# K transposed on TensorE for 48 units instead of 32, in halves through two PSUM banks

## The chip, the cores and the metric

The kernel runs on one core of a Trainium2 chip. The metric is the device time of that core in microseconds (us). Before the change three runs gave 1071.03, 1072.39 and 1073.0 us, a median of 1072.39; the profiled execution took 1071.12 us, with a profiled span of 1069.4 us at a granted TensorE clock of 0.999.

## The reference

Two attention blocks of the same shape, A and B, follow one another; their outputs stand side by side in the last dimension. For each block, with 16 batches, 16 heads, 144 query rows, 448 model columns, 512 cached keys and a head width of 256, all bf16:

```
q = (x @ wq) as 16 heads of 256 columns
scores = q @ k_cache^T / 16          for each batch and head
p = softmax(scores)
o = p @ v_cache
out = (o of the 16 heads, side by side) @ wo
```

## The kernel before

The work is cut into units: one unit is one batch and one head, 256 units for A and 256 for B, numbered through (U). A unit has 512 keys, 256 KB of K and 256 KB of V. Scores are computed with the keys on the partitions, so K is needed with the head width on the partitions, that is transposed, while V is used as it lies in memory.

One loop over i emits everything; in step i it emits, in this order,

- `t_tr(i+4)`: the transposes of K on TensorE, only for the first NNAT * UV = 32 units. Eight 128 x 128 transposes write one PSUM bank, `op_ps` seen as bf16 (`tr_ps`); then VectorE copies the first half and ScalarE the second half into `kt_sb` (L973). All three name the bank "op".
- `t_q(i+3)` and `t_evac_q(i+3)`: the Q projection (L1005) into `qp_ps`, two banks under the one name "qp", and its copy by VectorE into a slot of `qt_sb`. `q_pair` says for how many batches a unit's Q is made at once: 2 (288 columns, for this batch and the next), 1 (144 columns) or 0 (already made).
- `t_s(i+2)`: scores (L1038), in two halves of two key blocks, into one of three banks `s_ps` in turn; ScalarE takes the exp of each half (L1048) into `pt_sb`.
- `t_pv(i)` and `t_sum(i)`: the product with V (L1083) and the row sums by a matmul with ones (L1095), in one of two banks `ot_ps`. The sums come from partial sums that GpSimd made two steps earlier (`t_presum`, L1058 and L1062).
- `t_recip(i)` on ScalarE (a logarithm, L1106, and an exp, L1111), and on VectorE `t_check(i)` (two reductions over the sums, L1140) and `t_evac_ot(i)` (L1126), which scales the result into `ring`.
- pieces of the output projection (`t_op_piece`, L1182) into `op_ps`, from step 28 on (`OP_START`), at a rate that a running credit sets.

Each engine executes its own instructions in the order in which they were emitted. `_Sched.add` derives the waits: an operation waits for the last writers of what it reads, for the readers of what it overwrites, and, for each PSUM bank it names, for the last operation of every *other* engine on this bank:

```
        for bk in banks:
            last = self.banks.setdefault(bk, {})
            for e2, ev2 in last.items():
                if e2 != eng:
                    deps.append(ev2)
```

So two engines never work on one bank at the same time; whichever was emitted later waits.

All loads go through one queue, SyncE's, in an order that is written out for the first units (`START`, in which n, v, k, q, o and x stand for natural K of two units, V of two units, transposed K of 16 units, a part of wq, a part of wo, a group of x) and planned after it. Natural K (`t_load_n`, L954) and V (`t_load_v`, L946) share the nine slots of `v_sb`, two units in each; a load waits until the load nine places earlier has been used. Transposed K (`t_load_k`, L933) is a transposing DMA of 16 units, a window, into one of the two halves of `kt_sb`; window W holds units 16W to 16W + 15. A window's load waits until the scores of the units that lay there before are done. In the kernel before, windows 0 and 1 are made on TensorE and all from window 2 on come by transposing DMA.

Of the kernel before, what the change touches and what calls it, by code (L numbers as in the profile page):

```python
# [5 lines left out]
BF16 = mybir.dt.bfloat16  # L6
F32 = mybir.dt.float32
I32 = mybir.dt.int32
AF = mybir.ActivationFunctionType
# [3 lines left out]
PE, ACT, DVE, POOL, SP = "pe", "act", "dve", "pool", "sp"  # L13
# [739 lines left out]
def bass_concat_heads__mha_block_cached__gqa_block_cached__near_ridge_kernel(  # L753
# [16 lines left out]
    ins = (A_x, A_k_cache, A_v_cache, A_wq, A_wo, B_x, B_k_cache, B_v_cache, B_wq, B_wo)  # L770
# [6 lines left out]
    Bn, SQ, D = A_x.shape  # L777
    H, SK, DH = A_k_cache.shape[1], A_k_cache.shape[2], A_k_cache.shape[3]
# [4 lines left out]
    UV = 2  # L783
# [3 lines left out]
    NWO = 2 * H  # L787
# [5 lines left out]
    LQ, LS, LT = 3, 2, 4  # L793
    KW, KR = 16, 32
    NV, NXG = 9, 2
    NNAT = KR // UV
    assert KR % KW == 0 and NU % KW == 0
    XB = 4
    assert Bn % (NXG * XB) == 0 and H == KW
    NQT, NPT, NPS, NRI, NOST, NRUN = 11, 3, 2, 2, 2, 32  # L800
# [5 lines left out]
    LIM_EXP = 40  # L806


    START = ("n0 q0 x0 n1 v0 n2 v1 q1 n3 v2 n4 v3 n5 q2 n6 v4 n7 v5 o0 q3 n8 v6 n9 v7 o1 n10 v8 o2 n11 v9 n12 v10 "
             "n13 v11 n14 v12 n15 v13 v14 k2 v15 o3 v16 v17 o4 o5 v18 o6 v19 o7 v20 v21 v22 x1 k3")  # L810
    MID = ("k16 v127 v128 q0 v129 v130 q1 v131 q2 q3 v132 k17 v133 v134 v135 v136 v137 o0 o1 v138 o2 v139 o3 v140 o4 v141 "
           "o5 v142 o6 o7 k18")

# [2 lines left out]
    with contextlib.ExitStack() as es:  # L816
# [8 lines left out]
        wq_sb = sb("wq_sb", [128, 4, H * DH], BF16)  # L825
        wo_sb = sb("wo_sb", [128, NWO, D], BF16)
        ring = sb("ring", [128, NWO, RC], BF16)
        kt_sb = sb("kt_sb", [128, 8, KR * 128], BF16)
        v_sb = sb("v_sb", [128, NV, UV, 4 * DH], BF16)
        xt_sb = sb("xt_sb", [128, 4, NXG * XB * SQ], BF16)  # L830
        qt_sb = sb("qt_sb", [128, NQT, 2, SQ], BF16)
        pt_sb = sb("pt_sb", [128, NPT, 4, SQ], BF16)
        ones = sb("ones", [128, 128], BF16)
# [8 lines left out]
        qp_ps = ps("qp_ps", [128, 2, 512], F32)  # L842
        s_ps = [ps("s_ps%d" % i, [128, 512], F32) for i in range(3)]
        ot_ps = [ps("ot_ps%d" % i, [128, 512], F32) for i in range(2)]
        op_ps = ps("op_ps", [128, 512], F32)
        tr_ps = op_ps[:, :].bitcast(BF16)
        ident = ring[:, NWO - 1, 2 * 128:3 * 128]

        S = _Sched()
        sem_names = list(COMPUTE)  # L850
# [14 lines left out]
        def unit(U):  # L865
            pr, r = divmod(U, NU)
            b, h = divmod(r, H)
            return pr, b, h

        def t_init():  # L870
            def e0(v):
                return v.memset(stat[:, 0:2], 0.0)
            S.add(DVE, e0, writes=[("scr", 0)], name="statz")

            def e1(a):
                a.preload_act_table_set("natural_log_exp_and_others")
                return a.activation(stat[0:1, 1:2], stat[0:1, 0:1], AF.Exp)
            S.add(ACT, e1, reads=[("scr", 0)], writes=[("scr1", 0)], name="actwarm")

            def e2(v):  # L880
                return v.memset(wq_sb[0:64, 3, :], 0.0)
            S.add(DVE, e2, writes=[("wqz", 0)], name="wqz")

            def e4(g):
                return g.memset(ones[:], 1.0)
            S.add(POOL, e4, writes=[("ones", 0)], name="ones")

            def e5(g):
                return g.affine_select(ident, ones[:], pattern=[[1, 128]], compare_op=ALU.is_equal,
                                       fill=0.0, base=0, channel_multiplier=-1)  # L890
            S.add(POOL, e5, reads=[("ones", 0)], writes=[(("ring", 2, H - 1), -1)], name="ident")
            for W in range(NNAT * UV // KW):
                S.res[(("kt", W))] = _Res()
                S.res[(("kt", W))].version = W

        def t_load_wq(pr, hg):
            cols = slice(hg * 4 * DH, (hg + 1) * 4 * DH)
# [56 lines left out]
                return q.dma_start(v_sb[:, sl, :, :], src).then_inc(sems["v%d" % sl], 16)  # L954
            S.add(SP, e, writes=[(("v", sl), ("n", G))], dma_sem="v%d" % sl, name="n%d" % G)

        def t_tr(U):
            G, j = divmod(U, UV)
            sl = v_seq["n", G] % NV
            ko = U % KR * 128  # L960

            def e(t):
                ins = None
                for k in range(8):
                    ins = t.transpose(tr_ps[:, k * 128:(k + 1) * 128], v_sb[:, sl, j, k * 128:(k + 1) * 128], ident)  # L965
                return ins
            S.add(PE, e, reads=[(("v", sl), ("n", G)), (("ring", 2, H - 1), -1)], writes=[("opp", ("t", U))],
                  banks=["op"], name="TR%d" % U)
            for k, eng in ((0, DVE), (1, ACT)):
                def ev(g, k=k, eng=eng):  # L970
                    dst = kt_sb[:, 4 * k:4 * k + 4, ko:ko + 128]
                    src = tr_ps[:, k * 512:(k + 1) * 512].rearrange("p (c q) -> p c q", c=4)
                    return g.activation(dst, src, AF.Copy) if eng == ACT else g.tensor_copy(dst, src)  # L973
                S.add(eng, ev, reads=[("opp", ("t", U))], writes=[(("ktn", U % KR), 0)], banks=["op"],
                      name="etr%d.%d" % (U, k))

        def q_pair(U):

            b, h = unit(U)[1:]
            if h % 2 == 0:  # L980
                return 2 if b % 2 == 0 else 0
            j = b % (NXG * XB)
            return 1 if j in (0, NXG * XB - 1) else (2 if j % 2 else 0)

        q_slot, q_live = {}, {}
        for U in range(NT):
            for u in [u for u in q_live if u - LS < U - LQ]:
# [5 lines left out]
        def t_q(U):  # L993
            pr, b, h = unit(U)
            n = q_pair(U)
            xo = b % (NXG * XB) * SQ
            xr = sorted(set((pr * Bn + b + k) // XB for k in range(n)))
            hg = h // 4

            def e(t):  # L1000
                ins = None
                for dc in range(2):
                    for kc in range(4):
                        c0 = h * DH + dc * 128
                        ins = t.matmul(qp_ps[:, dc, 0:n * SQ], lhsT=wq_sb[:, kc, c0:c0 + 128],  # L1005
                                       rhs=xt_sb[:, kc, xo:xo + n * SQ], start=(kc == 0), stop=(kc == 3))
                return ins
            S.add(PE, e, reads=[(("wq", hg), pr), ("wqz", 0)] + [(("xt", XG % NXG), XG) for XG in xr],
                  writes=[("qp", ("q", U))], banks=["qp"], name="Q%d" % U)

        def t_evac_q(U):
            n = q_pair(U)
            us = [U + k * H for k in range(n)]
            a, b = q_slot[us[0]], q_slot[us[-1]]

            def e(v):
                if n == 1:
                    return v.tensor_copy(qt_sb[:, a, :, :], qp_ps[:, :, 0:SQ])  # L1018
                return v.tensor_copy(qt_sb[:, a:b + 1:b - a, :, :],  # L1019
                                     qp_ps[:, :, 0:2 * SQ].rearrange("p e (u q) -> p u e q", u=2))  # L1020
            S.add(DVE, e, reads=[("qp", ("q", U))], writes=[(("qt", q_slot[u]), u) for u in us], banks=["qp"],
                  name="eq%d" % U)

        def t_s(U):
            W = U // KW
            ksl = W % (KR // KW)
            ko = U % KR * 128
            qsl = q_slot[U]
            kn = [(("ktn", U % KR), 0)] if U < NNAT * UV else []
            psl = U % NPT  # L1030
            for k in range(2):
                bank = (2 * U + k) % 3

                def e(t, k=k, bank=bank):
                    ins = None
                    for c in (2 * k, 2 * k + 1):
                        for dc in range(2):
                            ins = t.matmul(s_ps[bank][:, (c % 2) * SQ:(c % 2 + 1) * SQ],  # L1038
                                           lhsT=kt_sb[:, 2 * c + dc, ko:ko + 128],
                                           rhs=qt_sb[:, qsl, dc, :], start=(dc == 0), stop=(dc == 1))  # L1040
                    return ins
                S.add(PE, e, reads=[(("qt", qsl), U), (("kt", ksl), W)] + kn, writes=[(("sp", bank), 2 * U + k)],
                      banks=["s%d" % bank], name="S%d.%d" % (U, k))
            for k in range(2):
                bank = (2 * U + k) % 3

                def x(a, k=k, bank=bank):
                    return a.activation(pt_sb[:, psl, 2 * k:2 * k + 2, :].rearrange("p b q -> p (b q)"),  # L1048
                                        s_ps[bank][:, 0:2 * SQ], AF.Exp, scale=DH ** -0.5)
                S.add(ACT, x, reads=[(("sp", bank), 2 * U + k)], writes=[(("pt", psl), U)], banks=["s%d" % bank],  # L1050
                      name="ex%d.%d" % (U, k))
# [238 lines left out]
        i = s_min  # L1290
        while True:
# [11 lines left out]
                t_store(stores.pop(0)[0])  # L1303
            u = i + LT
            if 0 <= u < NNAT * UV:
                t_tr(u)
            u = i + LQ
            if 0 <= u < NT and q_pair(u):
                t_q(u)
# [1 line left out]
            u = i + LS  # L1311
            if 0 <= u < NT:
                t_s(u)
            if -LS <= i < 0:
                t_presum(i + LS)
            u = i
# [122 lines left out]
```

## Time and profile before

| | |
|---|---|
| median time | 1072.39 us |
| TensorE busy | 1037.2 us, 97% |
| ScalarE, VectorE, GpSimd busy | 65%, 62%, 58% |
| TensorE busy from 0 to 20 us | 11.67 us |
| TensorE busy from 20 to 90 us | 60.01 us |
| TensorE busy from 90 to 130 us | 38.38 us |
| TensorE busy from 130 to 300 us | 168.57 us of 170 |
| PV of unit 0, of unit 28, of unit 46 start | 17.84, 91.25, 132.09 us |

In the profile a line number (L973) is that of the kernel's source as printed above. "Busy" of TensorE is the time covered by matmuls; since they are pipelined, eight of them that are listed with 0.66 us may start only 0.50 us before the next eight. A wait is listed as the idle time of an engine ahead of an instruction, with what ended it. The chain of work that ended last is followed back from the last instruction, at each step to what released it, so that it shows which operations set the time.

### The profile page before, as it was taken

How to read it: one execution, taken by the hardware profiler on the slowest of the kernel's cores; microseconds unless marked ns; L12 is line 12 of the kernel's file. 1: busy time of each engine (PE TensorE's matmuls, PEld its weight loads, DVE VectorE, ACT ScalarE, POOL GpSimd, SP SyncE). 2: the span in 40 equal slices, each digit the busy share in tenths (PEclk: the TensorE clock that was granted, in tenths of full speed). 3: DMA queues.
4: the chain of work that ended last, by engine and by line, in shares of the span. 5: the costliest groups of instructions: out<-in, count | busy, mean ns of one | idle time of the engine just before them, and what ended most of it. 6: DMA issues, size and time to landing. Idle time of an engine off the chain costs nothing.

```text
span 1069.4 us, 31680 instructions
## 1 busy us (share of the span) xinstructions
PE 1037.2 (97%) x12416; PEld 879.1 (82%) x12416; DVE 664.1 (62%) x2023; ACT 699.3 (65%) x2117; POOL 624.0 (58%) x1030
## 2 busy tenths in 40 slices
PE   6889899999999999999999999999999999999997
PEld 5778788888888888888888788888888888888885
DVE  4656566666666666666656656666666666666664
ACT  4666566667756666666756566666775666667674
POOL 2445555656655556665755556566675556666663
PEclk9999999999999999999999999999999999999999
DMA  9989999999999999999999999999999999999950
GB/s 314 353 229 330 244 287 278 289 303 277 300 253 288 257 283 247 303 276 276 263 307 339 278 292 279 280 311 274 289 270 285 288 296 283 281 283 238 275 191 13
DMA packets 603038, 294.10 MB, mean 275 GB/s; under 512 B 516864, under 2 KB 529664, under 8 KB 602880
## 3 DMA queue, kind: packets, MB, share of 16 engines
q1 hardware_dynamic: 602880, 291.99, 109.0%
q8 instruction: 99, 1.62, 0.6%
q14 instruction: 59, 0.48, 0.1%
HBM read 157.29 MB, written 4.13 MB: 151 GB/s over the span
## 4 chain that ended last, share of the span: by engine, by line
PE 91%; ACT 3%; DVE 3%; DMA 2%; SPq 1%; issue 0%; DVEq 0%
PE ot_ps L1083 23%; PE s_ps L1038 23%; PE qp_ps L1005 22%; PE op_ps L1182 20%; PE ot_ps L1095 3%; ACT kt_sb L973 1%; ACT pt_sb L1048 1%; DVE run_sb L1140 1%; DVE ring L1126 1%; DMA v_sb<-in_B_v_cache_dram 1%; DVE kt_sb L973 1%; ACT rinv_sb L1106 1%; PE qp_ps L1182 1%; DMA v_sb<-in_A_v_cache_dram 0%; DMA v_sb<-in_A_k_cache_dram 0%; SPq L923 0%
## 5 line engine op out<-in xcount | busy, mean ns | idle before, releaser
L1058 POOL TENSOR_TENSOR pp_sb<-pt_sb 128x288 f32<-128x288 bf16 x512 | 373.2, 729 | 357.7 <-ACT pt_sb L1048 334.2
L1048 ACT ACTIVATE pt_sb<-s_ps 128x288 bf16<-128x288 f32 x1024 | 364.1, 408 | 256.6 <-PE s_ps L1038 256.2
L1140 DVE TENSOR_REDUCE run_sb<-ot_ps 1x1 bf16<-1x144 f32 x1024 | 262.2, 293 | 337.0 <-ACT rinv_sb L1106 336.9
L1038 PE MATMUL s_ps<-qt_sb,kt_sb 128*128 128x144 bf16 x4096 | 339.9, 226 | 5.0 <-DMA kt_sb<-in_A_k_cache_dram 2.5
L1083 PE MATMUL ot_ps<-pt_sb,v_sb 128*128 128x144 bf16 x4096 | 339.7, 226 | 2.2 <-DMA v_sb<-in_B_v_cache_dram 1.7
L1038 PEld LDWEIGHTS s_ps<-qt_sb,kt_sb 128*128 128x128 bf16 x4096 | 288.4, 98 | 52.8 <-issue 5.6
L1005 PE MATMUL qp_ps<-xt_sb,wq_sb 128*128 128x288 bf16 (+1 forms) x2304 | 299.8, 273 | 4.1 <-DMA xt_sb<-in_A_x_dram 1.8
L1062 POOL TENSOR_TENSOR ps_sb<-pp_sb 128x144 bf16<-128x144 f32 x512 | 250.2, 489 | 73.7 <-PE ot_ps L1095 0.6
L1182 PE MATMUL op_ps<-wo_sb,ring 128*128 128x448 bf16 x1120 | 284.6, 352 | 0.4 <-DVE ring L1126 0.4
L1005 PEld LDWEIGHTS qp_ps<-xt_sb,wq_sb 128*128 128x128 bf16 x2304 | 210.5, 98 | 83.4 <-issue 2.0
L1083 PEld LDWEIGHTS ot_ps<-pt_sb,v_sb 128*128 128x128 bf16 x4096 | 274.0, 98 | 3.1 <-DMA v_sb<-in_B_v_cache_dram 2.0
L1126 DVE TENSOR_TENSOR ring<-ot_ps,rinv_sb 128x288 bf16<-128x288 f32 (+2 forms) x640 | 231.0, 375 | 0.0
L1019 DVE CAST qt_sb<-qp_ps 128x576 bf16<-128x576 f32 x224 | 168.9, 754 | 49.2 <-PE qp_ps L1005 44.7
L1106 ACT ACTIVATE rinv_sb<-ot_ps 128x144 f32<-128x144 f32 x512 | 149.4, 292 | 50.8 <-PE ot_ps L1095 6.3
L1111 ACT ACTIVATE rinv_sb<-rinv_sb 128x144 f32<-128x144 f32 x512 | 165.3, 323 | 16.2
L1095 PE MATMUL ot_ps<-ps_sb,ones 128*128 128x144 bf16 x512 | 115.7, 226 | 0.0
L1182 PEld LDWEIGHTS op_ps<-wo_sb,ring 128*128 128x128 bf16 x1120 | 93.8, 98 | 21.8 <-DVE ring L1126 0.8
L1095 PEld LDWEIGHTS ot_ps<-ps_sb,ones 128*128 128x128 bf16 x512 | 50.1, 98 | 0.0
L973 ACT ACTIVATE kt_sb<-op_ps 128x512 bf16<-128x512 bf16 x32 | 19.1, 597 | 35.8 <-DVE kt_sb L973 35.8
L965 PE MATMUL op_ps<-ring,v_sb 128*128 128x128 bf16 x256 | 21.0, 228 | 15.5 <-ACT kt_sb L973 10.3
L965 PEld LDWEIGHTS op_ps<-ring,v_sb 128*128 128x128 bf16 x256 | 15.5, 101 | 20.7 <-ACT kt_sb L973 15.0
L1018 DVE CAST qt_sb<-qp_ps 128x288 bf16<-128x288 f32 x64 | 28.1, 439 | 4.2 <-PE qp_ps L1005 4.0
(19 smaller groups left out, 51.2 us busy)
## 6 DMA issues: line engine op xcount, KB each, us to landing
v_sb<-in_A_v_cache_dram SPq DMA_DIRECT2D x128, 512.0 KB, 7.1
v_sb<-in_B_v_cache_dram SPq DMA_DIRECT2D x128, 512.0 KB, 7.1
v_sb<-in_A_k_cache_dram SPq DMA_DIRECT2D x16, 512.0 KB, 9.1
out_dram<-ost_sb SPq DMA_DIRECT2D x36, 112.0 KB, 5.9
wo_sb<-in_A_wo_dram SPq DMA_DIRECT2D x8, 448.0 KB, 9.0
wo_sb<-in_B_wo_dram SPq DMA_DIRECT2D x8, 448.0 KB, 8.8
wq_sb<-in_A_wq_dram SPq DMA_DIRECT2D x4, 768.0 KB, 9.5
wq_sb<-in_B_wq_dram SPq DMA_DIRECT2D x4, 768.0 KB, 10.1
```

The costliest lines, as they stand in the source:

```text
L1005: ins = t.matmul(qp_ps[:, dc, 0:n * SQ], lhsT=wq_sb[:, kc, c0:c0 + 128], rhs=xt_sb[:, kc, xo:xo + n * SQ], start=(kc == 0), stop=(kc == 3))
L1019: return v.tensor_copy(qt_sb[:, a:b + 1:b - a, :, :], qp_ps[:, :, 0:2 * SQ].rearrange("p e (u q) -> p u e q", u=2))
L1038: ins = t.matmul(s_ps[bank][:, (c % 2) * SQ:(c % 2 + 1) * SQ], lhsT=kt_sb[:, 2 * c + dc, ko:ko + 128], rhs=qt_sb[:, qsl, dc, :], start=(dc ...
L1048: return a.activation(pt_sb[:, psl, 2 * k:2 * k + 2, :].rearrange("p b q -> p (b q)"), s_ps[bank][:, 0:2 * SQ], AF.Exp, scale=DH ** -0.5)
L1058: return g.tensor_tensor(pp_sb[:, :, :], pt_sb[:, psl, 0:2, :], pt_sb[:, psl, 2:4, :], op=ALU.add)
L1062: return g.tensor_tensor(ps_sb[:, sl, :], pp_sb[:, 0, :], pp_sb[:, 1, :], op=ALU.add)
L1083: ins = t.matmul(ot_ps[ob][:, dc * SQ:(dc + 1) * SQ], lhsT=v_sb[:, vsl, j, c * DH + dc * 128:c * DH + (dc + 1) * 128], rhs=pt_sb[:, sl, c, ...
L1095: return t.matmul(ot_ps[ob][:, 2 * SQ:3 * SQ], lhsT=ones[:, :], rhs=ps_sb[:, sl, :], start=True, stop=True)
L1111: return a.activation(rinv_sb[:, sl, :], ln, AF.Exp, scale=-1.0)
L1126: ins = v.tensor_tensor(ring[:, 2 * h:2 * h + 2, r0:r0 + q1 - q0], ot_ps[ob][:, 0:2 * SQ].rearrange("p (c q) -> p c q", c=2)[:, :, q0:q1], ...
L1140: return v.tensor_reduce(run_sb[0:1, k, j:j + 1], ot_ps[ob][0:1, 2 * SQ:3 * SQ], axis=AX.X, op=op)
L1182: ins = t.matmul(acc[0:m, 0:D], lhsT=ring[:, c, col0:col0 + m], rhs=wo_sb[:, c, :], start=(c == first), stop=(c == last))
```

## The change

The transposes on TensorE go on for 48 units, three windows, so that the first window that comes by transposing DMA is window 3. They are split: `t_tr(U, 0)` writes four transposes into bank 2 of the scores and VectorE copies them, `t_tr(U, 1)` writes the other four into the second bank of `qp_ps` and ScalarE copies them. Neither copy shares a bank with the other, so they may run at once. `t_tr(U, 0)` stays at the head of the step, `t_tr(U, 1)` stands between the scores and PV. To keep these banks free for it, scores of the first 48 units use banks 0 and 1 alone, and Q of these units is made for one batch at a time, in the first bank of `qp_ps`; the two banks have names of their own now ("qp", "qp1"). For the 16 units after them the even heads, too, make a single Q. The identity for the transposes moves from the ring to the last slot of `qt_sb`. The order of the first loads has eight more natural loads of K, no window 2, and x1 earlier.

```diff
-    NNAT = KR // UV
+    NNAT = 3 * KW // UV
...
-    START = ("n0 q0 x0 n1 v0 n2 v1 q1 n3 v2 n4 v3 n5 q2 n6 v4 n7 v5 o0 q3 n8 v6 n9 v7 o1 n10 v8 o2 n11 v9 n12 v10 "
-             "n13 v11 n14 v12 n15 v13 v14 k2 v15 o3 v16 v17 o4 o5 v18 o6 v19 o7 v20 v21 v22 x1 k3")
+    START = ("n0 q0 x0 n1 v0 n2 q1 v1 n3 q2 n4 v2 n5 v3 q3 n6 v4 n7 v5 n8 v6 o0 n9 v7 n10 v8 o1 n11 v9 n12 v10 o2 n13 "
+             "v11 n14 v12 o3 n15 v13 x1 n16 v14 o4 n17 v15 n18 v16 o5 n19 v17 n20 v18 o6 n21 v19 n22 v20 o7 n23 v21 v22 "
+             "k3")
...
-        tr_ps = op_ps[:, :].bitcast(BF16)
-        ident = ring[:, NWO - 1, 2 * 128:3 * 128]
+        tr_ps = (s_ps[2][:, :].bitcast(BF16), qp_ps[:, 1, :].bitcast(BF16))
+        ident = qt_sb[:, NQT - 1, 0, 0:128]
...
-        def t_tr(U):
+        def t_tr(U, k):
...
+            bank, eng = (("s2", DVE), ("qp1", ACT))[k]
+            key = (("sp", 2), "qp1")[k]
...
-                for k in range(8):
-                    ins = t.transpose(tr_ps[:, k * 128:(k + 1) * 128], v_sb[:, sl, j, k * 128:(k + 1) * 128], ident)
+                for c in range(4):
+                    a = (4 * k + c) * 128
+                    ins = t.transpose(tr_ps[k][:, c * 128:(c + 1) * 128], v_sb[:, sl, j, a:a + 128], ident)
...
         def q_pair(U):
             b, h = unit(U)[1:]
+            if U < NNAT * UV:
+                return 1
+            if U < NNAT * UV + H and h % 2 == 0:
+                return 1
...
-                        ins = t.matmul(qp_ps[:, dc, 0:n * SQ], lhsT=wq_sb[:, kc, c0:c0 + 128],
+                        acc = qp_ps[:, dc, 0:2 * SQ] if n == 2 else qp_ps[:, 0, dc * SQ:(dc + 1) * SQ]
+                        ins = t.matmul(acc, lhsT=wq_sb[:, kc, c0:c0 + 128],
...
-                bank = (2 * U + k) % 3
+                bank = k if U < NNAT * UV else (2 * U + k) % 3
...
             if 0 <= u < NNAT * UV:
-                t_tr(u)
+                t_tr(u, 0)
...
             if 0 <= u < NT:
                 t_s(u)
+            u = i + LT
+            if 0 <= u < NNAT * UV:
+                t_tr(u, 1)
```

More of the change, by code (lines that the diff above doesn't have):

```diff
@@ L845, in bass_concat_heads__mha_block_cached__gqa_block_cached__near_ridge_kernel @@
         op_ps = ps("op_ps", [128, 512], F32)
-        tr_ps = op_ps[:, :].bitcast(BF16)
-        ident = ring[:, NWO - 1, 2 * 128:3 * 128]
+        tr_ps = (s_ps[2][:, :].bitcast(BF16), qp_ps[:, 1, :].bitcast(BF16))
+        ident = qt_sb[:, NQT - 1, 0, 0:128]
+        id_key = (("qt", NQT - 1), -1)
         S = _Sched()
@@ L890, in e5 @@
                                        fill=0.0, base=0, channel_multiplier=-1)
[L891 to L894, printed above, removed]
+            S.add(POOL, e5, reads=[("ones", 0)], writes=[id_key], name="ident")
         def t_load_wq(pr, hg):
@@ L960, in t_tr, with ev @@
             ko = U % KR * 128
+            kt_key = ("kt", U // KW % (KR // KW))
+            if k == 0 and U % KW == 0:
+                S.res[kt_key] = _Res()
+                S.res[kt_key].version = U // KW
+            bank, eng = (("s2", DVE), ("qp1", ACT))[k]
+            key = (("sp", 2), "qp1")[k]
             def e(t):
                 ins = None
-                for k in range(8):
-                    ins = t.transpose(tr_ps[:, k * 128:(k + 1) * 128], v_sb[:, sl, j, k * 128:(k + 1) * 128], ident)
-                return ins
[L967 to L975, printed above, removed]
+                for c in range(4):
+                    a = (4 * k + c) * 128
+                    ins = t.transpose(tr_ps[k][:, c * 128:(c + 1) * 128], v_sb[:, sl, j, a:a + 128], ident)
+                return ins
+            S.add(PE, e, reads=[(("v", sl), ("n", G)), id_key], writes=[(key, ("t", U))], banks=[bank],
+                  name="TR%d.%d" % (U, k))
+            def ev(g):
+                dst = kt_sb[:, 4 * k:4 * k + 4, ko:ko + 128]
+                src = tr_ps[k][:, 0:512].rearrange("p (c q) -> p c q", c=4)
+                return g.activation(dst, src, AF.Copy) if eng == ACT else g.tensor_copy(dst, src)
+            S.add(eng, ev, reads=[(key, ("t", U))], writes=[(("ktn", U % KR), U)], banks=[bank],
+                  name="etr%d.%d" % (U, k))
         def q_pair(U):
             b, h = unit(U)[1:]
+            if U < NNAT * UV:
+                return 1
+            if U < NNAT * UV + H and h % 2 == 0:
+                return 1
             if h % 2 == 0:
@@ L983, in q_pair @@
             return 1 if j in (0, NXG * XB - 1) else (2 if j % 2 else 0)
+        q_banks = ["qp", "qp1"]
         q_slot, q_live = {}, {}
@@ L1008, in t_q @@
             S.add(PE, e, reads=[(("wq", hg), pr), ("wqz", 0)] + [(("xt", XG % NXG), XG) for XG in xr],
-                  writes=[("qp", ("q", U))], banks=["qp"], name="Q%d" % U)
+                  writes=[(bk, ("q", U)) for bk in q_banks[:n]], banks=q_banks[:n], name="Q%d" % U)
         def t_evac_q(U):
@@ L1017, in e @@
                 if n == 1:
-                    return v.tensor_copy(qt_sb[:, a, :, :], qp_ps[:, :, 0:SQ])
+                    return v.tensor_copy(qt_sb[:, a, :, :], qp_ps[:, 0, 0:2 * SQ].rearrange("p (e q) -> p e q", e=2))
                 return v.tensor_copy(qt_sb[:, a:b + 1:b - a, :, :],
                                      qp_ps[:, :, 0:2 * SQ].rearrange("p e (u q) -> p u e q", u=2))
-            S.add(DVE, e, reads=[("qp", ("q", U))], writes=[(("qt", q_slot[u]), u) for u in us], banks=["qp"],
+            S.add(DVE, e, reads=[(bk, ("q", U)) for bk in q_banks[:n]],
+                  writes=[(("qt", q_slot[u]), u) for u in us], banks=q_banks[:n],
                   name="eq%d" % U)
@@ L1028, in t_s @@
             qsl = q_slot[U]
-            kn = [(("ktn", U % KR), 0)] if U < NNAT * UV else []
+            kn = [(("ktn", U % KR), U)] if U < NNAT * UV else []
             psl = U % NPT
             for k in range(2):
-                bank = (2 * U + k) % 3
+                bank = k if U < NNAT * UV else (2 * U + k) % 3
                 def e(t, k=k, bank=bank):
@@ L1044, in t_s @@
             for k in range(2):
-                bank = (2 * U + k) % 3
+                bank = k if U < NNAT * UV else (2 * U + k) % 3
                 def x(a, k=k, bank=bank):
```

## The prediction, made before the changed kernel was run

> **What bounds the kernel now.** I read the shares and the 40 slices first: TensorE is busy 97% of the span and ScalarE, the next, 65%; only the first slices have room (8 to 9 tenths, then 9 to the end). So a saving elsewhere is worth what it frees on TensorE, and only the start has something to free. I call step i the turn of the loop that ends with `t_pv(i)`; it also holds the transposes of unit i+4, Q of unit i+3 and scores of unit i+2. The waits between 20 and 90 us, that is steps 1 to 27 (columns: who waits, for whom, us in total, times, longest):
>
> ```profile
> ACT kt_sb L973 <- DVE kt_sb L973: 23.9, 26, 0.9
> PEld op_ps L965 <- ACT kt_sb L973: 13.6, 24, 1.2
> PE op_ps L965 <- ACT kt_sb L973: 9.2, 13, 1.0
> ```
>
> The second copy out of the transpose bank (ScalarE) starts only after the first (VectorE) has ended, and the next unit's transposes start after both. The chain that ended last, here between 36 and 46 us (start, length, what), shows it as a closed loop; one turn:
>
> ```profile
> 38.31 0.51 DVE run_sb L1140 x2
> 38.82 0.36 DVE ring L1126
> 39.19 0.34 DVE kt_sb L973
> 39.53 0.02 issue
> 39.55 0.60 ACT kt_sb L973
> 40.15 0.60 ACT pt_sb L1048 x2
> 40.75 0.19 ACT rinv_sb L1106
> 40.95 0.02 issue
> 40.97 0.51 DVE run_sb L1140 x2
> ```
>
> 40.97 - 38.31 = 2.66 us a unit, with no TensorE in it: VectorE's checks (L1140), evacuation (L1126) and K copy (L973), ScalarE's K copy, exps and logarithm, and round again. What TensorE does in two such turns (start, length, idle before):
>
> ```profile
> 40.20 0.62 PE L965 MATMUL op_ps<-ring,v_sb 128*128 128x128 bf16 x8 [0.47 <-ACT kt_sb L973]
> 40.66 1.14 PE L1005 MATMUL qp_ps<-xt_sb,wq_sb 128*128 128x288 bf16 x8
> 41.64 0.66 PE L1038 MATMUL s_ps<-qt_sb,kt_sb 128*128 128x144 bf16 x8
> 42.14 0.66 PE L1083 MATMUL ot_ps<-pt_sb,v_sb 128*128 128x144 bf16 x8
> 42.64 0.23 PE L1095 MATMUL ot_ps<-ps_sb,ones 128*128 128x144 bf16 x1
> 42.86 0.62 PE L965 MATMUL op_ps<-ring,v_sb 128*128 128x128 bf16 x8
> 43.32 0.66 PE L1005 MATMUL qp_ps<-xt_sb,wq_sb 128*128 128x144 bf16 x8
> 43.82 0.66 PE L1038 MATMUL s_ps<-qt_sb,kt_sb 128*128 128x144 bf16 x8
> ```
>
> From start to start: transposes 0.45 us, a pair's Q 0.98, a single Q 0.50, scores 0.50, PV 0.50, sum 0.06. The queue of loads has one late piece in this stretch: the transposing load of K for units 48 to 63 (second line, start and time of its issue) stands behind the one for units 32 to 47 and all that this one held up, and TensorE waited for it (third line).
>
> ```profile
> 68.84 18.90 SPq L933 DMA_TRANSPOSE kt_sb<-in_A_k_cache_dram  x1
> 109.67 17.55 SPq L933 DMA_TRANSPOSE kt_sb<-in_A_k_cache_dram  x1
> 130.88 0.66 PE L1038 MATMUL s_ps<-qt_sb,kt_sb 128*128 128x144 bf16 x8 [2.45 <-DMA kt_sb<-in_A_k_cache_dram]
> ```
>
> **What the Trainium skill says.** "PSUM — Partial Sum Buffer", Specifications: ScalarE and VectorE can read PSUM in parallel at full rate as long as they don't meet in one bank. This is what the two banks are for; the trace has only the opposite case, ScalarE waiting 23.9 us for VectorE. "TensorE: Matmul & The Clock Gate", section "Wait — 56ns, not 53.3ns?": matmuls start N cycles of 2.4 GHz plus 2.5 ns apart; for N of 144 that is 62.5 ns, and eight take 0.50 us in the trace, so it agrees, and two single Qs (1.00) cost hardly more than a pair (0.98). "Advanced Engine Details and Errata", "X-Bar Transpose (TRN2)": a transposing DMA is as fast as a plain one. Here it isn't: a 4.19 MB window took 21 us to land (200 GB/s), while plain loads moved up to 391 GB/s in the slices before 60 us.
>
> **The change part by part.**
> 1. *Two banks.* ScalarE's copy waits only for its own four transposes, VectorE's for the other four. The 2.66 us loop is cut. What bounds a step then? TensorE's own work: 0.45 + 0.50 (Q) + 0.50 + 0.50 + 0.06 = 2.01 us. ScalarE, start to start from the same stretch: two exps 0.58, copy 0.49, logarithm 0.34, reciprocal 0.32 = 1.73. VectorE: checks 0.44, evacuation 0.36, copy 0.33, Q copy 0.43 = 1.56. GpSimd 0.73 + 0.49 = 1.22. A new loop goes over two steps: sum matmul to the end of the Q copy behind it took 2.15 us (32.41 to 34.56: logarithm, checks, evacuation, K copy, Q copy), then Q, which waits for its bank, then 1.72 us of TensorE to the sum matmul of that step; with some 0.1 for the waits, 3.97 / 2 = 1.99 us a step. So TensorE is the bound, by very little. I take 2.05 us (bounds 2.01 and, if the engines don't overlap their operations, 2.3).
>    PV of unit 0 to PV of unit 28 took 17.84 to 91.25 = 73.4 us. With 28 x 2.05 = 57.4: **-16.0 us**.
> 2. *Sixteen more units transposed*, in steps 28 to 43, beside the output projection, where TensorE is full. The one in step 28 is in the 57.4 already; 15 x 0.45 = **+6.8**. The copies they add to VectorE and ScalarE lie inside the 2.5 us of such a step.
> 3. *Q single.* Until PV of unit 46, steps 28 to 46 lose 8 pairs (7.84) and gain 17 singles (8.5): **+0.7**. After it the even heads of batch 3, which a pair had served before, have 7 more singles: **+3.5**. Ahead of PV 0, Q of unit 2 is single: **-0.5** (that of unit 0 is hidden by the wait for the second K load, to 12.22 us).
> 4. *K window 2 no longer by DMA.* The 18.9 us in which the queue issued it, with all V loads and wo behind, go; eight plain loads of 0.52 MB come. Window 3 is now issued behind `v22`, which waits for PV 35. From there to the scores of unit 48 are 8 steps of 2.5, two of 1.95 and Q of unit 49: about 25 us; it lands after 21, and `v23` behind it some 22.5 after its issue (17.6 for the issue, 4.8 to land as before), needed at 25.5. So both waits of before, 2.45 and 0.54, go: **-3.0**. The margin of 3 to 4 us is thin (landing up to 26 us occurs in the trace).
> 5. *Loads for faster steps.* Two loads of 0.52 MB in two steps of 2.05 us are 256 GB/s, with wo 310; the queue gave 326 to 391 there. A slot comes free 8 steps (16 us) ahead of its need, and a K load took 9.1 us. In the first ten steps the bytes moved by each time (5.3 MB by 18.8 us, 8.2 by 26.3, 10.9 by 33.8) put K loads 3, 4 and 6 within 1 us of their need. I take **+1.0** (0 to 3).
> 6. *Transposes through bank 2 of the scores.* Scores of one unit take banks 0 and 1 and wait for the exps of the unit before, which end half a step earlier: nothing. The move of the identity: nothing, it is made beside the wait for the first load.
>
> Sum: -16.0 + 6.8 + 0.7 + 3.5 - 0.5 - 3.0 + 1.0 = **-7.5**. After batch 3 the work is the same and TensorE stays the bound, so it reaches the end: 1072.4 - 7.5 = 1064.9.
>
> **The rivals.**
> *Loads late (chance 0.16).* Window 3 takes 24 to 26 us, or x1, now issued in step 19 (9.3 us of issue in the trace, 5.2 for x0), delays K load 16. For it: the thin margins of 4 and 5. Against: the queue is emptier without window 2. It costs 2 to 4 us: 1068.5.
> *ScalarE and VectorE stay the bound (0.08).* By mean durations ScalarE's step is 2 x 0.408 + 0.597 + 0.292 + 0.323 = 2.03; with 0.25 of waiting 2.3 us: 28 x 0.25 = 7 us given back, 1071.9. Against: start to start they fit into 1.73.
> *Slower (0.09).* Nine slots for two streams hold the steps at the old pace, loads taking the place of the copies: then only the additions remain, 16 x 0.45 = 7.2, + 0.7 + 3.5 - 3.0 = +8.4, that is 1081. For it: 48 units instead of 32 now need twice the plain loads. Against: before 60 us no V load was waited for, with the queue at its full rate only while it filled the slots.
> *The forecast* 0.62, and 0.05 for more than it (steps at 2.01, no wait for loads: 1062.5).
>
> **How the numbers follow.** The likeliest is 1064.9. Best bound: 2.01 a step (-1.1), no late load (-1), a smoother start (-1 to -2): 1061. On the other side the range takes in late loads and part of the slow loop: 1070. Outside are some 0.03 below and 0.15 above. Faster by over 0.2% (2.1 us): forecast, better, late loads, 0.83; within: the bound loop and a piece of late loads, 0.07; slower 0.10.
>
> **What would show it.** Step 1: waits of ScalarE's K copy for VectorE near zero, and PV starts 2.0 to 2.1 us apart until unit 28 (around 75.5 us). Steps 2 and 3: 384 transposes; 80 single Qs in the first half where 32 were; PV 46 near 121 us. Step 4: no wait for a K window at unit 48. Step 5: TensorE's waits for K loads under 2 us beyond the first two. It is wrong if a wait of Q or of the transposes for VectorE appears in every step, or if waits for loads sum to several us.

## The result, and the profile after

The changed kernel took 1066.2 us (median of 4 runs, 1063.18 to 1067.92) against 1072.7 us before (a fourth run of the kernel before, 1074.44 us, raised its median): a ratio of 0.9936 with a 95% interval of 0.9907 to 0.9966. Two later sets, run beside other kernels, gave 1064.06 us (6 runs) against 1072.95 us and 1066.25 us (5 runs) against 1074.53 us, with ratios of 0.9922 (0.9906 to 0.9938) and 0.9922 (0.9909 to 0.9934). So it is 0.6 to 0.8% faster, 6.5 to 8.9 us by the medians; 7.5 us had been forecast. The profiled span fell from 1069.4 to 1061.4 us.

The chain that ended last, in the changed kernel from 56 to 59 us (start, length, what):

```profile
56.30 0.22 PE s_ps L972 x4
56.52 0.50 PE qp_ps L1018 x8
57.02 0.50 PE s_ps L1052 x8
57.52 0.22 PE qp_ps L972 x4
57.75 0.50 PE ot_ps L1097 x8
58.25 0.06 PE ot_ps L1109
58.31 0.22 PE s_ps L972 x4
```

One turn is 58.31 - 56.30 = 2.01 us, and every piece of it is TensorE; in the kernel before a turn took 2.66 us and had no TensorE in it. The groups of the pages say the same of the K copies, first ScalarE's in the kernel before, then both in the changed one (busy, mean ns | idle before, what ended it):

```profile
L973 ACT ACTIVATE kt_sb<-op_ps 128x512 bf16<-128x512 bf16 x32 | 19.1, 597 | 35.8 <-DVE kt_sb L973 35.8
```

```profile
L980 ACT ACTIVATE kt_sb<-qp_ps 128x512 bf16<-128x512 bf16 x48 | 28.9, 603 | 8.5 <-PE qp_ps L972 8.5
...
L980 DVE COPY kt_sb<-s_ps 128x512 bf16<-128x512 bf16 x48 | 19.5, 405 | 6.3 <-PE s_ps L972 6.2
```

A copy costs what it cost, 603 ns and 405 ns, but ScalarE's now waits for TensorE alone, 8.5 us for 48 copies, where 32 had waited 35.8 us for VectorE.

Where the time went, by the start of PV of some units, in us:

| kernel | PV 0 | PV 8 | PV 28 | PV 46 | PV 56 | PV 64 | PV 256 | span |
|---|---|---|---|---|---|---|---|---|
| before | 17.84 | 39.00 | 91.25 | 132.09 | 152.53 | 168.73 | 549.56 | 1069.4 |
| changed | 18.59 | 35.48 | 75.67 | 120.43 | 143.37 | 160.58 | 539.97 | 1061.4 |
| changed, second profile | 18.25 | 35.38 | 75.56 | 120.33 | 143.27 | 160.47 | 539.86 | 1063.4 |
| changed, third profile | 18.31 | 35.31 | 75.49 | 120.25 | 143.20 | 160.40 | 540.01 | 1064.7 |

The gain is 15.6 us at PV 28, 11.7 at PV 46, 9.2 at PV 56 and 8.2 at PV 64; it is 9.6 at PV 256, the first of block B, and 8.0, 6.0 or 4.7 at the end. The three profiles of the changed kernel agree within 0.2 us from PV 8 to PV 256, so what scatters between them lies behind it.

It lies in the loads of block B. TensorE waited for loads of K and V of B for 4.1 us in the profile of before, and for 3.1, 6.0 and 7.5 us in the three of the changed kernel. Before has one wait more, which the three of the changed kernel lack and which makes up most of the 1.2 to 1.4 us that the gain grows by between PV 64 and PV 256:

```profile
541.78 1.14 PE L1005 MATMUL qp_ps<-xt_sb,wq_sb 128*128 128x288 bf16 x8 [1.28 <-DVE ring L1126]
```

It is listed under VectorE, but a piece of B's wq had landed 0.09 us ahead of its end, at 541.69 us. The same wait, with the same 0.09 us, is in six other profiles below and missing in four; what decides that is open. The one wait of the first profile of the changed kernel:

```profile
566.88 1.14 PE L1097 MATMUL ot_ps<-pt_sb,v_sb 128*128 128x144 bf16 x8 [3.05 <-DMA v_sb<-in_B_v_cache_dram]
```

Eight matmuls listed with 1.14 us instead of 0.66 are slow ones. Two stretches of 6 us, of the first profile and of the third, where the wait was 2.94 us (columns: stretch, its length, PE, PEld, VectorE, ScalarE and GpSimd busy with counts, granted TensorE clock, DMA share, GB/s):

```profile
566.00:572.00 6.00, 5.12 (x31) 3.98 (x32) 1.63 (x4) 1.22 (x4) 0.49 (x1) 0.50 1.05 390
```

```profile
566.00:572.00 6.00, 5.18 (x65) 4.53 (x66) 2.87 (x8) 2.70 (x9) 1.79 (x4) 1.00 1.03 382
```

After nearly the same wait the clock was 0.50 in one and 1.00 in the other, and TensorE did 31 matmuls against 65. In the kernel before, the waits there were 1.04, 2.43 and 0.62 us, with the clock at 1.00 behind each.

### The profile page after: what moved, and what is told of

It reads as the page before. It is cut to its first block, busy times and chain, and to the rows that moved or that the text cites. A ratio compares the mean times of both kernels' runs of the same rounds, so it can differ in the third digit from the quotient of the medians.

```text
span 1061.4 us, 32383 instructions
## 1 busy us (share of the span) xinstructions
PE 1043.1 (98%) x12736; PEld 895.5 (84%) x12736; DVE 670.9 (63%) x2063; ACT 706.4 (67%) x2133; POOL 625.6 (59%) x1030
## 4 chain that ended last, share of the span: by engine, by line
PE 97%; DMA 2%; SPq 1%; DVE 0%; issue 0%; ACT 0%; DVEq 0%
PE s_ps L1052 24%; PE ot_ps L1097 24%; PE qp_ps L1018 24%; PE op_ps L1196 20%; PE ot_ps L1109 3%; DMA v_sb<-in_A_k_cache_dram 1%; PE s_ps L972 1%; PE qp_ps L972 1%; PE qp_ps L1196 1%; DMA v_sb<-in_B_v_cache_dram 1%; SPq L922 0%; SPq L923 0%; DVE ost_sb L1217 0%; SPq L902 0%; DVE run_sb L1154 0%
## 5 line engine op out<-in xcount | busy, mean ns | idle before, releaser
L1018 PE MATMUL qp_ps<-xt_sb,wq_sb 128*128 128x288 bf16 (+1 forms) x2496 | 305.3, 266 | 3.6 <-DMA xt_sb<-in_A_x_dram 3.6
L1018 PEld LDWEIGHTS qp_ps<-xt_sb,wq_sb 128*128 128x128 bf16 x2496 | 218.8, 98 | 79.0 <-issue 4.4
L1032 DVE CAST qt_sb<-qp_ps 128x576 bf16<-128x576 f32 x200 | 151.1, 755 | 41.7 <-PE qp_ps L1018 37.6
L1031 DVE CAST qt_sb<-qp_ps 128x288 bf16<-128x288 f32 x112 | 49.2, 439 | 9.4 <-PE qp_ps L1018 8.8
L980 ACT ACTIVATE kt_sb<-qp_ps 128x512 bf16<-128x512 bf16 x48 | 28.9, 603 | 8.5 <-PE qp_ps L972 8.5
L972 PE MATMUL s_ps<-qt_sb,v_sb 128*128 128x128 bf16 x192 | 19.4, 226 | 6.2 <-DMA v_sb<-in_A_k_cache_dram 6.1
L980 DVE COPY kt_sb<-s_ps 128x512 bf16<-128x512 bf16 x48 | 19.5, 405 | 6.3 <-PE s_ps L972 6.2
```

Source lines behind the costliest of these rows:

```text
L1018: ins = t.matmul(acc, lhsT=wq_sb[:, kc, c0:c0 + 128], rhs=xt_sb[:, kc, xo:xo + n * SQ], start=(kc == 0), stop=(kc == 3))
L1032: return v.tensor_copy(qt_sb[:, a:b + 1:b - a, :, :], qp_ps[:, :, 0:2 * SQ].rearrange("p e (u q) -> p u e q", u=2))
```

## The experiments

In all of them the ratio is to the kernel before, on the same chip. The changed kernel itself ran beside them only in two groups: with one bank, two banks and 32 units, and single Q, and with the two kernels under the last heading. Elsewhere a comparison with it is one between chips, and such differences of 2 or 3 us in the whole are not explained unless a profile shows where they arise. "In step" below means that PV starts were 2.01 us apart.

### The changed kernel again

> The changed kernel unaltered, on the chip and in the rounds of the three others, so that they can be set against it. The four runs so far gave 1063.2 to 1067.9 us. Theory (the transposes' loop is cut, TensorE bounds the stretch): 1066 us, ratio to before 0.991 to 0.997, PV of units 1 to 28 again 2.01 us apart. If the gain of the first comparison was scatter of runs, the ratio comes out above 0.998.

Measured: 1064.06 us, ratio 0.9922 (0.9906 to 0.9938), in step from PV 8 to PV 28. The gain is not scatter.

### One bank instead of two

```diff
-        tr_ps = (s_ps[2][:, :].bitcast(BF16), qp_ps[:, 1, :].bitcast(BF16))
+        tr_ps = s_ps[2][:, :].bitcast(BF16)
...
-                t_tr(u, 0)
+                t_tr(u)
```

Here `t_tr(u)` is that of the kernel before, with bank "s2" in place of "op".

> The changed kernel with only the split undone: the eight transposes of a unit stand together at the head of the step and write one bank (bank 2 of the scores), VectorE copies the first half and ScalarE, after it, the second. 48 units, single Q and the order of loads stay. Theory: the loop of 2.66 us a unit comes back for steps 1 to 28 (28 x (2.66 - 2.01) = +18 us) and holds the steps 28 to 43 slightly too (2.66 against 2.5 on average, +2): 1086 us, slower than before by some 13. Rival (the gain came from single Q, the order of loads or the K window by plain loads, the split does nothing): 1066 us, PV 2.0 us apart.

Measured: 1084.24 us, ratio 1.0108 (1.0087 to 1.0129). PV 28 came at 92.25 us. The waits from 20 to 90 us:

```profile
ACT kt_sb L977 <- DVE kt_sb L977: 23.8, 26, 0.9
PEld s_ps L969 <- ACT kt_sb L977: 16.9, 26, 0.7
PE s_ps L969 <- ACT kt_sb L977: 12.1, 26, 0.5
```

These are the lines of before, to 0.1 us in the first, and a turn of the chain took 2.66 us again (check of sums to check of sums, first line to last):

```profile
43.73 0.51 DVE run_sb L1151 x2
...
44.97 0.60 ACT kt_sb L977
45.57 0.60 ACT pt_sb L1059 x2
...
46.39 0.51 DVE run_sb L1151 x2
```

So without the split the rest of the change costs 11.3 us; with it, in the same set, the kernel gains 8.9. The split is worth 20.2 us, of which some 19.5 are there by PV 46 (139.78 us for 120.33), that is in the 44 steps with transposes and PV.

### Two banks, 32 units

```diff
-    NNAT = 3 * KW // UV
+    NNAT = 2 * KW // UV
...
-            if U < NNAT * UV + H and h % 2 == 0:
+            if U < NNAT * UV + H and h % 2 == 1:
```

with the order of the first loads as before the change.

> The changed kernel with only the extension undone: transposes in two banks for 32 units instead of 48, window 2 by transposing DMA and the order of the first loads as before the change; Q is single for the first 32 units and for the odd heads of batch 2. Theory (the extension pays for itself by keeping loads in time): PV 28 near 76 us as in the changed kernel, then 6.8 us less transposing, but the queue is held for 18 us by window 2: V of units 30 and 31 1 to 2 us late, and window 3, issued near 98 us and landing near 120, 6 to 8 us late for unit 48; in all 1067 to 1069 us. Rival (two banks carry the whole gain and 16 more units are pure cost): 1059 us, no wait for K above 1 us.

Measured: 1070.23 us, ratio 0.9975 (0.9967 to 0.9984). The waits for windows 2 and 3 and for V behind them are there, 4.8 us together (1.79 at window 3, where 6 to 8 had been expected), but a wait had been missed: PV 28 came at 79.47 us, not 76, since Q of unit 8 waited for wq (start, length, idle before):

```profile
30.50 1.12 PE L1017 MATMUL qp_ps<-xt_sb,wq_sb 128*128 128x144 bf16 x8 [2.52 <-DMA wq_sb<-in_A_wq_dram]
...
85.26 0.66 PE L1051 MATMUL s_ps<-qt_sb,kt_sb 128*128 128x144 bf16 x8 [0.64 <-DMA kt_sb<-in_A_k_cache_dram]
87.46 0.67 PE L1096 MATMUL ot_ps<-pt_sb,v_sb 128*128 128x144 bf16 x8 [1.54 <-DMA v_sb<-in_A_v_cache_dram]
...
124.83 0.66 PE L1051 MATMUL s_ps<-qt_sb,kt_sb 128*128 128x144 bf16 x8 [1.79 <-DMA kt_sb<-in_A_k_cache_dram]
126.33 1.12 PE L1096 MATMUL ot_ps<-pt_sb,v_sb 128*128 128x144 bf16 x8 [0.83 <-DMA v_sb<-in_A_v_cache_dram]
```

With this wait in it, the run doesn't say what the extension to 48 units is worth. The same kernel with wq as early as in the changed one does.

```diff
-    START = ("n0 q0 x0 n1 v0 n2 v1 q1 n3 v2 n4 v3 n5 q2 n6 v4 n7 v5 o0 q3 n8 v6 ...
+    START = ("n0 q0 x0 n1 v0 n2 q1 v1 n3 q2 n4 v2 n5 v3 q3 n6 v4 n7 v5 n8 v6 o0 ...
```

> The two-bank kernel with 32 units again, now with the changed kernel's order of the first loads up to V of units 26 and 27 (wq parts 1 to 3 early), then window 2 and the rest as before the change. With the old order Q of unit 8 waited 2.52 us for wq, and TensorE's granted clock was 0.57 in the 4 us after. Theory: that wait and the slow stretch behind it, 2.5 + 1.7 = 4.2 us, go; the waits for windows 2 and 3 and the V behind them (4.8 us together) stay; 1066 us, level with the changed kernel: the extension's 6.8 us of transposing bought back about as much in waits. Rival (with the loads in a fitting order the extension is pure cost): 1062 us or less. Other rival (the extension is needed): 1069 us or more.

Measured: 1066.08 us, ratio 0.9932 (0.9908 to 0.9955); PV 28 at 75.03 us, no wait for wq. TensorE waited 1.25 us for window 2, not at all for window 3, and 1.76 and 1.62 us for V behind them, 4.6 us. It is level with the changed kernel. At PV 128 (285.69 us) it is 0.9 us ahead of it, and it loses that again to a wait of 2.41 us for B's wq, which the changed kernel's profiles don't have. So the extension buys back in waits about what its transposes cost, and no gain of it can be measured. What the new order with wq early is worth beside the two banks can: PV 28 comes 4.4 us earlier than with the old one, and the whole is 4 us shorter.

### Single Q alone, on the kernel before

```diff
             b, h = unit(U)[1:]
+            if U < 3 * KW:
+                return 1
+            if U < 3 * KW + H and h % 2 == 0:
+                return 1
```

> The kernel before with only the pairing of Q changed as in the change: single Q for the first 48 units and for the even heads of batch 3. Theory (single Q costs no more per column, it only moves eight units' Q from the stretch where TensorE waits to one where it is full): steps to unit 28 unchanged at 2.66 us, then +0.7 and +3.5, so 1076 to 1077 us, 0.4% slower than before. Rival (single Q helps by itself, since each copy by VectorE is shorter and the loop through it turns faster): steps below 2.6 us and 1070 us or less.

Measured: 1077.84 us, ratio 1.0052 (1.0033 to 1.0071). PV 28 at 91.35 us, 0.10 from before: in the stretch that the copies bound, less work for TensorE brings nothing. The cost comes later, when batch 3 has to do itself what pairs had done for it.

### x1 in its old place

```diff
-             "... n15 v13 x1 n16 ... v22 k3"
+             "... n15 v13 n16 ... v22 x1 k3"
```

> The changed kernel with x1 back in its old place, just ahead of K window 3 in the queue of loads. Theory (window 3 has a margin of about 3 us: issued at 95.0 us, landed 116.9, needed 119.9): the issue of x1 takes 6.5 to 8.5 us in front of it, so window 3 lands at 123.5 to 125.5 us and the scores of unit 48 wait 3.5 to 5.5 us, V of units 46 and 47 perhaps 0.5 more; 1068 to 1070 us. Rival (the place of x1 is indifferent, the queue or the transposing load has more room than that): 1064 us, no wait at unit 48.

Measured: 1066.72 us, ratio 0.9951 (0.9934 to 0.9968). SyncE's issues and the one wait of TensorE near unit 48:

```profile
94.81 2.95 SPq L922 DMA_TRANSPOSE xt_sb<-in_A_x_dram  x1
97.80 1.56 SPq L923 DMA_TRANSPOSE xt_sb<-in_A_x_dram  x1
99.41 17.14 SPq L932 DMA_TRANSPOSE kt_sb<-in_A_k_cache_dram  x1
...
121.40 0.67 PE L1097 MATMUL ot_ps<-pt_sb,v_sb 128*128 128x144 bf16 x8 [1.01 <-DMA v_sb<-in_A_v_cache_dram]
```

A miss in size: x1 took 4.5 us of issue, not 6.5, and window 3, issued 4.4 us later than in the changed kernel, landed 19.9 us after its issue instead of 21.9, at 119.3, ahead of its need; 3.5 to 5.5 us of waiting had been expected. Only V behind it was late, by 1.0 us. PV 46 is 1.0 us later than in the changed kernel; the rest of the difference in the whole lies after PV 56, where this profile waited 8.3 us for loads of B.

### Both copies on VectorE

```diff
-            bank, eng = (("s2", DVE), ("qp1", ACT))[k]
+            bank, eng = (("s2", DVE), ("qp1", DVE))[k]
```

> The changed kernel with both K copies on VectorE, still in two banks. Theory (what the change removed is that one engine's copy waited for the other's, and that the next transposes waited for both; which engine empties the second bank matters little): VectorE's step becomes 1.56 + 0.33 = 1.89 us, ScalarE's 1.73 - 0.49 = 1.24, both under TensorE's 2.01; the second copy is done before the logarithm that starts the loop over two steps; PV still 2.01 us apart, 1064 to 1066 us. Rival (two engines emptying at once is what carries the gain, or the loop over VectorE has no room at all): steps of 2.15 us or more, 1068 us or more.

Measured: 1067.65 us, ratio 0.9953 (0.9937 to 0.9970); in step, PV 28 at 75.32 us and PV 56 at 143.03, both earlier than in the changed kernel. From 20 to 75 us VectorE was busy 51.94 us of 55, ScalarE 36.24:

```profile
20.00:75.00 55.00, 55.00 (x907) 55.00 (x905) 51.94 (x165) 36.24 (x110) 33.55 (x56) 1.00 1.06 363
```

So the stretch doesn't need two engines emptying at once; it needs copies that don't wait for each other in one bank. Both copies on one engine out of one bank was not tried, nor two engines in one bank without the rule that makes one wait for the other. So it stays open how much the second bank does by itself and how much the end of the wait between two engines. The whole is above the forecast of 1064 to 1066, 3.6 us above the 1064.06 of the changed kernel and 1.4 above the 1066.25, but this profile has 8.0 us of waits after 150 us, all for loads of B (1.72 of them listed under VectorE's `ring`, ended 0.09 us after a piece of wq had landed), and nothing in the code differs there; I put the difference down to them, which one profile can't prove.

### TensorE kept busy while it waits

```diff
+            if u in (0, 2):
+                t_warm({0: 16, 2: 14}[u])
             if 0 <= u < NNAT * UV:
                 t_tr(u, 0)
+            if u == 1:
+                t_warm(30)
```

`t_warm(n)` makes n transposes of the identity into `op_ps`.

> The changed kernel with 60 extra transposes of the identity into the idle projection bank, ahead of and between the first loads, to keep TensorE busy while it waits. In the changed kernel the instructions between 12.4 and 16.4 us took twice their later time (eight 144-column matmuls 0.96 us, later 0.50), and PV 0 came 0.75 us later than before the change. Theory: they run at full rate now and PV 0 starts 1 to 1.9 us earlier, but K loads 4 and 6 (landing at 25.7 and 34.0 us) then set the steps, so PV 8 stays near 35.4 us and the whole at 1064 us. Rival (the slow start costs its full time): PV 8 and the whole 1 to 2 us earlier, 1062.5 us.

Measured: 1067.53 us, ratio 0.9955 (0.9939 to 0.9972). PV 0 came at 16.50 us, 2.1 earlier, Q of unit 1 took 0.50 us instead of 0.96; but PV 8 came at 35.24, 0.24 earlier. The 2 us were lost again in waits, the last of them for the K load of units 12 and 13; the first, of Q of unit 4, is listed under `ring`, but the piece of wq that it needs had landed 0.14 us before, at 18.49 us, as the K loads had before the two others:

```profile
18.63 0.66 PE L1026 MATMUL qp_ps<-xt_sb,wq_sb 128*128 128x144 bf16 x8 [1.18 <-DVE ring L1148]
...
21.10 0.38 PE L980 MATMUL s_ps<-qt_sb,v_sb 128*128 128x128 bf16 x4 [0.53 <-DMA v_sb<-in_A_k_cache_dram]
33.80 0.38 PE L980 MATMUL s_ps<-qt_sb,v_sb 128*128 128x128 bf16 x4 [0.21 <-DMA v_sb<-in_A_k_cache_dram]
```

In the changed kernel that load had let TensorE go on at 34.04 us. The start is bound by the loads, and a faster TensorE only waits for them. That the whole is 3.5 us above the 1064 expected arises elsewhere: PV 56 came at 143.13 us, 0.24 earlier than in the changed kernel, and behind it are 6.2 us of waits for loads of B and a granted clock of 0.50 in the 6 us after one of them.

### 64 units

```diff
-    NNAT = 3 * KW // UV
+    NNAT = 4 * KW // UV
...
-            if U < NNAT * UV + H and h % 2 == 0:
+            if U < NNAT * UV + H and h % 2 == 1:
```

and natural loads of K 24 to 31 in place of window 3.

> The changed kernel with the extension driven on: 64 units transposed on TensorE instead of 48, window 3 by eight more plain loads, the first transposing load is window 4; Q single for 64 units and for the odd heads of batch 4. Theory (16 units of transposes cost 16 x 0.45 = 7.2 us of a full TensorE, and are worth it only where they take away a late window; window 3 was in time): 1071 to 1072 us. Rival (each window taken from the transposing DMA gives something back, since it relieves the queue): 1064 us or less.

Measured: 1072.97 us, ratio 1.0000 (0.9992 to 1.0009): the whole gain of the change spent. It is 6.7 to 8.9 us over the sets of the changed kernel; at PV 80 (200.80 us), ahead of what scatters, 7.4 us, where 16 x 0.45 = 7.2 had been expected. Taking a window from the transposing DMA gives nothing back by itself.

### Halves at the head, and V ahead of window 17

Beside a third set of the changed kernel:

> The changed kernel unaltered, to stand beside the two others on the same chip. So far 1063.7 to 1065.2 us in one round of runs and 1063.2 to 1067.9 in another; the waits for loads of B near 567 and 608 us summed to 3.0 us in one profile and 6.1 in the other. Expected 1064 to 1067 us.

Measured: 1066.25 us (1064.46 to 1067.12).

```diff
                 t_tr(u, 0)
+                t_tr(u, 1)
```

(and the later call removed)

> The changed kernel with both halves of a unit's transposes at the head of the step, still in two banks and emptied by two engines; only the place of the second half changes. Theory (the two banks matter, not the place): the second half waits for ScalarE's copy of the unit before, long done, TensorE has the same 2.01 us of work a step, PV 2.01 us apart, the same time as the changed kernel within 2 us. Rival (the second half is where it is because ScalarE's copy would otherwise stand in front of its exps and hold the step): steps of 2.1 us or more, 2.5 us or more over the changed kernel.

Measured: 1066.7 us, ratio 0.9926 (0.9913 to 0.9939), in step from PV 8 on. The place of the second half is indifferent.

```diff
-    MID = ("... v132 k17 v133 v134 v135 ..."
+    MID = ("... v132 v133 v134 k17 v135 ..."
```

> The changed kernel with the two loads of V for units 266 to 269 moved ahead of K window 17 in the queue, to take away the wait for V near 567 us (3.0 us in the changed kernel's profile), where V stands behind a transposing load whose issue took 26.9 us. Theory: window 17 is issued 8 us later and still lands before unit 272 needs it; the wait goes and the kernel gains 2 to 3 us on the changed one run beside it, 1061 to 1064 us. Rival (the queue is full there and the wait only moves to window 17 or to the V behind it): the same time as the changed kernel.

Measured: 1064.64 us (1063.73 to 1068.91), ratio 0.9919 (0.9904 to 0.9934). The wait near 567 us is gone; those near 605 us, for the next window and V behind it, stay:

```profile
604.92 0.97 PE L1052 MATMUL s_ps<-qt_sb,kt_sb 128*128 128x144 bf16 x8 [2.76 <-DMA kt_sb<-in_B_k_cache_dram]
607.57 1.14 PE L1097 MATMUL ot_ps<-pt_sb,v_sb 128*128 128x144 bf16 x8 [1.68 <-DMA v_sb<-in_B_v_cache_dram]
```

1.6 us less than the changed kernel beside it, with ranges that overlap: the wait went, a gain is not shown.

## Why the prediction was right

1. *Two banks.* Forecast 2.05 us a step with 2.01 as the bound, and 57.4 us from PV 0 to PV 28 with 1.0 more for late loads; measured 2.01 from PV 8 on and 57.1 with the waits for loads in it. That TensorE takes over "by very little" shows in the loop over two steps, estimated at 2.15 us from the sum matmul to the end of the Q copy behind it:

```profile
46.03 0.23 PE L1109 MATMUL ot_ps<-ps_sb,ones 128*128 128x144 bf16 x1
...
47.81 0.43 DVE L1031 CAST qt_sb<-qp_ps 128x288 bf16<-128x288 f32 x1
...
48.32 0.66 PE L1018 MATMUL qp_ps<-xt_sb,wq_sb 128*128 128x144 bf16 x8
```

   47.81 + 0.43 - 46.03 = 2.21 us, and the Q that needs the bank starts 0.08 us later. TensorE was due then anyway: its wait is not listed.
   The skill's statement on two engines in two banks ("PSUM — Partial Sum Buffer", Specifications) agrees with the trace, though not by the two K copies: these meet for over 0.05 us in 3 of 48 units, since VectorE's is about done when ScalarE's transposes are.

```profile
47.48 0.40 DVE L980 COPY kt_sb<-s_ps 128x512 bf16<-128x512 bf16 x1
47.86 0.60 ACT L980 ACTIVATE kt_sb<-qp_ps 128x512 bf16<-128x512 bf16 x1
```

   What ScalarE's copy does meet is VectorE's Q copy out of the other bank of `qp_ps` (47.81 us above), and both keep their lengths, 0.60 and 0.43 us, whether they meet or not. So the gain is not that the two copies run at once; it is that neither waits for the other.
2. *Sixteen more units, single Q, windows in time.* From PV 28 to PV 46 the forecast was 40.84 - 3.0 + 6.8 + 0.7 = 45.3 us; measured 44.8. No wait for window 3 is listed at unit 48, and it had landed 3 us ahead, the margin forecast as 3 to 4. The 64-unit run gives the price of 16 more units again, 7.4 us at PV 80.
3. *The start* did not come as forecast: -0.5 for the single Q of unit 2, but PV 0 was 0.75 us later. Around Q of unit 0 TensorE waited 3.57 and 0.88 us, and it ran at half speed until 16.4 us. Whether the change did this is open: with the same opening PV 0 came at 17.02 us in the 64-unit run and at 19.21 with x1 in its old place, and there is one profile of before, with 17.84. The run that kept TensorE busy shows that the slow stretch costs nothing: K loads set PV 8.
   So the fit at PV 28, 75.67 us measured and some 75.7 by the sum, is in part luck: PV 0 was 1.25 us later than the sum has it, and the way from there 1.3 us shorter. (Two readings at the start were off and bear on nothing: the first slice of the page is 6 tenths busy, not 8, and one slice before 60 us has 400 GB/s, not 391.)
4. *Late loads.* Forecast +1.0 up to unit 14, K loads 4 and 6 among those within 1 us; measured 0.32 and 0.18 us for just these two, half of the forecast.
5. *Afterwards the work is the same.* Right of the work, not of the time. From PV 46 to the end +3.5 was forecast; the three profiles had +3.7, +5.8 and +7.1. Of this +2.5 was there by PV 56, five single Qs, and +3.5 by PV 64, all seven: this term came as forecast. The rest, 0.2 to 3.6 us, is what the waits for loads of B and the slow clock behind some of them differ from those of before: 1.2 to 1.4 us less up to PV 256, for the wait for wq that before has and the three profiles lack, and 1.6 to 4.9 more behind it. The sum had taken these as unchanged. They are what the spread of the runs is made of, as far as profiles show it, and that the end came out within some 1.5 us of the forecast is luck as far as they go.

The forecast was 7.5 us and the sets gave 6.5 to 8.9. The rivals: late loads cost less than 1 us in the stretch that the change touches, and the several us of waits for loads of B were there before; ScalarE and VectorE did not stay the bound, and even with both copies on VectorE the steps held; the slots fed the faster steps. One point of the change's own purpose was not in the forecast: that the extension to 48 units can be left out at no measurable cost, if the first loads keep the order with wq early.

## What to carry to other kernels

Look for a closed loop in the chain of waits: if the busiest engine doesn't appear in one turn, the length of the turn is a latency, and cutting one link frees the engine until its own work, or the next loop, takes over; both can be worked out beforehand from start-to-start times. If two engines empty one bank in turn, and one waits for the other, give each piece a bank of its own; here it made no difference to the steps whether one engine or two emptied them. Then follow what a faster stretch asks of the loads, since here one wait of 2.5 us for a weight, with the slow clock behind it, cost 4 us, half of the gain.

## What the runs showed of the hardware

After a wait of TensorE its granted clock can fall to half for some us: 0.50 from 566 to 572 us with a wait of 3.05 us in it (changed kernel), 0.57 from 30 to 34 us with the end of one of 2.52 us (two banks, 32 units). It need not: it stayed at 1.00 after one of 2.94 us (changed kernel, third profile) and after one of 3.48 us (both copies on VectorE, the 6 us from 568.85). So the length of the wait alone doesn't decide it; what does is open. Nor does the listed clock show every slow stretch: from 12 to 16 us of the changed kernel it is 1.00, while eight 144-column matmuls took 0.96 us, later 0.50.

A transposing load of 4.19 MB held SyncE for 16 to 27 us of issue, and every load behind it; in the changed kernel it landed 2.0 to 3.7 us after the end of its issue (21.9 us after its start where the issue took 19.8, 27.1 where it took 25.1), 18.7 to 29.0 us after its start. At 145 to 224 GB/s it is slower than the loads from 20 to 75 us, nearly all plain, with 363 GB/s together. "Advanced Engine Details and Errata", "X-Bar Transpose (TRN2)", has them equal; the measurement decides.
